# Two PSUM banks handed out by hand, centring ahead of the last masked score, and the variance inside a feature tile

## The chip, the core and the metric

The kernel runs on one core of a Trainium2 chip. Five engines work from queues of their own, each in order: TensorE (PE in the profile, its weight loads PEld), VectorE (DVE), ScalarE (ACT), GpSimd (POOL) and SyncE (SP), which here only issues DMAs. They wait for each other through semaphores. The metric is the time on the device in microseconds (us), the median of several runs. Matrix products accumulate in PSUM; a PSUM bank here is a tile of 128 partitions by 512 fp32 values.

## The reference

Attention over 8 batches of 8 heads with 576 tokens and head size 64, in which only scores close to the row's maximum count, and then a feed-forward block with a layer norm in front. All in fp32 (the feed-forward weights come in as float64):

```python
scores = matmul(q, k^T) / 8
keep   = scores >= max(scores) - tau
attn   = exp(scores - max(scores)) where keep, else 0
x      = concat_heads((attn / sum(attn)) @ v)               # (8, 576, 512)
mu, var = mean(x), mean((x - mu)**2)                        # over the 512 features
out    = x + max(((x - mu) / sqrt(var + 1e-6) * g_ln) @ w_ch1, 0) @ w_ch2
```

`w_ch1` is 512 x 2048, `w_ch2` 2048 x 512.

## The kernel before

**Slots and groups.** The attention runs in 72 slots, nine to a batch: for each pair of heads two slots of 256 queries, and one (the fifth) for the last 64 queries of all heads. The feed-forward block runs in 16 groups of 288 tokens, two to a batch (even group first). `x` lies with features on partitions, so a group's input is four chunks of 128 x 288. Program order is order on every engine (`tc.manual_schedule()`, L147); there is no scheduler that moves anything afterwards. The main loop (L1089) writes out a slot in four quarters, and `second_part(n, i)` (L1006) puts as many steps of the feed-forward generator between them as a budget allows. So TensorE's queue is one stream, in which products of both halves alternate.

**A slot.** `scores` (L388) fills two score tiles, VectorE takes negated maxima (L419), ScalarE exponentials (L432, four of 128 x 576), VectorE masks and sums each (L439, four, `weights`), POOL divides (L455), VectorE transposes (L529), and the result goes through a DRAM scratch tile and back (`turn_blocks`, `fetch`) and is multiplied with V in the next slot (L598, L608). Each of the two score tiles is three banks long (L376).

**Two more banks.** All other products use one pool, `ps_ff`, with one tag and two buffers (L76): whoever asks for a tile gets the buffer that was handed out longest ago, and waits until all that used it is done. In the feed-forward half they are, in order:

- `mean_of(g)` (L659): one product with a matrix of 1/512, which gives the mean in all partitions. While a group's segments run, a flag holds it back, and it is issued 12 steps into the last segment (L962 to L966).
- `centre(g)` (L666): VectorE subtracts the mean from the four chunks (L673) and so writes `xc`, which the first products of the group read. For an odd group this stands at the end of a slot, for an even one in the third quarter, behind all masked scores. At which quarter these are called is set in `group_ready` (L1036).
- `first_part(g)` (L776): 16 tiles of the hidden layer, each of four products into one bank (`p1`), which ScalarE empties with a relu (L796). On the way ScalarE squares `xc`, POOL adds up the squares, and after a later tile one product with the same matrix gives the variance (L809), from which ScalarE makes the inverse root: a bias row (L816), Ln (L817), Exp (L818). VectorE refines it (`root`, L734).
- `second_quarters` (L842) for groups 1 to 15: the second product by a scheme with seven products of half size; each of the seven segments fills a bank in 32 steps, and ScalarE copies it out (L887). Group 0 has a plain second product (`second_plain`).

The two lines that hand out a tile and hold the mean back:

```python
    ps_ff = ctx.enter_context(tc.tile_pool(name="ps_ff", bufs=2, space=bass.MemoryType.PSUM))   # L76
        for _ in range(12):                                                                     # L962
            yield next(last)
```

In the first slots (batch 0) the weights are still being converted from float64 by all engines, and the attention's transposes (`tp`, `tr`) and products with V (`pv`) use the same two banks.

Of the kernel before, what the change touches and what calls it, by code (L numbers as in the profile page):

```python
# [18 lines left out]
def kernel(  # L19
# [53 lines left out]
    dram = ctx.enter_context(tc.tile_pool(name="dram", bufs=3, space=bass.MemoryType.DRAM))  # L73
    ffn = ctx.enter_context(tc.tile_pool(name="ffn", bufs=2))
    ps_sc = ctx.enter_context(tc.tile_pool(name="ps_sc", bufs=1, space=bass.MemoryType.PSUM))
    ps_ff = ctx.enter_context(tc.tile_pool(name="ps_ff", bufs=2, space=bass.MemoryType.PSUM))  # L76

    tau_sb = consts.tile([128, 1], F32, name="tau_sb")
    scl_sb = consts.tile([128, 1], F32, name="scl_sb")
# [351 lines left out]
                yield es, thr  # L431
            nc.scalar.activation(es[:, i], blocks[i], func=AF.Exp, bias=neg[:, i : i + 1])  # L432

    def weights(es, thr, divide):


        den = small.tile([128, 4], F32, tag="den", name="den")
        for i in range(4):
            nc.vector.scalar_tensor_tensor(  # L439
                out=es[:, i], in0=blocks[i], scalar=thr[:, i : i + 1], in1=es[:, i],  # L440
                op0=ALU.is_ge, op1=ALU.mult, accum_out=den[:, i : i + 1],
            )
# [26 lines left out]
    def turn_weights(s, es, diags):  # L469


        em, er = turned_tiles(s)
        for i in range(4):
            if i:
                yield
            tp = ps_ff.tile([128, J, 128], F32, tag="ff", name="tp")
            for c in range(J):
                product(
                    tp[:, c], lhsT=es[:, i, c * 128 : (c + 1) * 128], rhs=diags[i],
                    start=True, stop=True,  # L480
                )
            if s == HP:
                nc.scalar.copy(
                    em[:, :, :, 32 * i : 32 * i + 32].rearrange("p a c x -> p c a x"),
                    tp.rearrange("p c (a x) -> p c a x", a=4),
                )
            else:
                h, j = divmod(i, 2)
                nc.scalar.copy(  # L489
                    em[:, 2 * j : 2 * j + 2, :, 64 * h : 64 * h + 64].rearrange("p a c x -> p c a x"),  # L490
                    tp.rearrange("p c (a x) -> p c a x", a=2),
                )
        tr = ps_ff.tile([128, 2, 128], F32, tag="ff", name="tr")
        for i in range(4):
            rest = es[:, i, J * 128 :]
            if s == HP:
                to = tr.rearrange("p a (b x) -> p (a b) x", b=2)[:, i]
                for half in range(2):
                    at = slice(64 * half, 64 * half + 64)
                    nc.tensor.matmul(to[at], lhsT=rest, rhs=diags[i][:, at], start=True, stop=True)  # L500
            else:
                h, j = divmod(i, 2)
                nc.tensor.matmul(
                    tr[64 * j : 64 * j + 64, h], lhsT=rest, rhs=diags[i], start=True, stop=True
                )
# [66 lines left out]
    def values_of(b, s, turned_weights):  # L572
# [2 lines left out]
        at_once = b == 0 and s <= HP  # L575
        pv = pv_behind
        if at_once:
            both = ps_ff.tile([128, 2, 128], F32, tag="ff", name="pv")
            pv = [both[:, j] for j in range(2)]
        if s == HP:  # L580
            outs = [
# [77 lines left out]
    def mean_of(g):  # L659
        if banks_taken[0]:  # L660
            waiting_mean.append(g)
            return
        means[g] = ps_ff.tile([128, TOK], F32, tag="ff", name="mean")
        product(means[g], lhsT=avg_sb, rhs=sums.pop(g), start=True, stop=True)

    def centre(g):  # L666
        nonlocal issued
        while waiting_mean:
            issued += next(queue[0])[1]
        xc = centred[g] = ffn.tile([128, NK, TOK], F32, tag="xc", bufs=1, name="xc")  # L670
        mean = means.pop(g)
        for c in range(NK):
            nc.vector.tensor_tensor(  # L673
                out=xc[:, c], in0=groups[g][:, c], in1=mean, op=ALU.subtract
            )

# [99 lines left out]
    def first_part(g):  # L776
# [6 lines left out]
        for d in range(ND):  # L783
            while conversion.carried < 4 * (d // 4 + 1):
                yield 0, 0
            while d == ND - 2 and len(rooted) <= g and not plain:
                run_all(aside)
            p1 = ps_ff.tile([128, TOK], F32, tag="ff", name="p1")
            for c in range(NK):
                product(  # L790
                    p1, lhsT=w1_sb[c][:, d * 128 : (d + 1) * 128], rhs=xc[:, c],
                    start=(c == 0), stop=(c == NK - 1),
                )
                if c < NK - 1:
                    yield 1, 1
            nc.scalar.activation(hidden[:, d], p1, func=AF.Relu)  # L796
            next(sums_of, None)
            yield 2, 1
            if sq is None and d and (part > 1 or d == ND // 2 - 1):
# [2 lines left out]
                nc.scalar.activation(sq, xc, func=AF.Square)  # L802
                for c in range(1, NK):
                    nc.gpsimd.tensor_tensor(out=sq[:, 0], in0=sq[:, 0], in1=sq[:, c], op=ALU.add)
            elif sq is not None and rb is None and (
                d >= squared + (7 if plain else 3) and part > (0 if plain else 1)
                or d == ND - NK - 1
            ):
                var = ps_ff.tile([128, TOK], F32, tag="ff", name="var")  # L809
                product(var, lhsT=avg_sb, rhs=sq[:, 0], start=True, stop=True)  # L810
                rb = ffn.tile([128, TOK], F32, tag="rb", bufs=2, name="rb")
                two = [sq[:, c] for c in (2, 3)]
                if plain:
                    two = [ffn.tile([128, HM, HT], F32, tag="part", bufs=4, name="two") for _ in two]
                    two = [t.rearrange("p m t -> p (m t)") for t in two]
                nc.scalar.activation(two[0], var, func=AF.Identity, bias=eps_sb)  # L816
                nc.scalar.activation(rb, two[0], func=AF.Ln)  # L817
                nc.scalar.activation(rb, rb, func=AF.Exp, scale=-0.5)  # L818
                aside.append(lambda: root(rb, *two))
                yield 1, 1  # L820
        for _ in sums_of:
            pass
        return rb

    def second_plain(g, rb):
        for m in range(NK):
            p2 = ps_ff.tile([128, TOK], F32, tag="ff", name="p2")
            for d in range(ND):
                while conversion.carried <= conversion.n1 + 4 * m + d // 4:
                    yield 0, 0  # L830
# [11 lines left out]
    def second_quarters(g, rb):  # L842
# [29 lines left out]
                eng.tensor_tensor(out=out[at], in0=in0[at], in1=in1[at], op=op)  # L872

        def segment(weights, rhs, out=None):
            bank = ps_ff.tile([128, HM, HT], F32, tag="ff", name="seg")
            for d in range(HD):
                for m in range(HM):
                    at, end = (d, m), (HD - 1, HM - 1)
                    product(
                        bank[:, m], lhsT=weights[:, m, d], rhs=rhs[:, d],  # L880
                        start=at == (0, 0), stop=at == end,
                    )
                    if at != end:
                        yield 2, 0.5
            if out is None:
                out = ffn.tile([128, HM, HT], F32, tag="part", bufs=4, name="part")
            nc.scalar.copy(out, bank)  # L887
            return out

        def last_tiles(weights, rhs):  # L890


            for m in range(HM):
                bank = ps_ff.tile([128, HT], F32, tag="ff", name="end")
                for d in range(HD):
                    product(
                        bank, lhsT=weights[:, m, d], rhs=rhs[:, d],
                        start=d == 0, stop=d == HD - 1,
                    )
# [4 lines left out]
                dve.tensor_tensor(out=z, in0=bank, in1=rb[:, late], op=ALU.mult)  # L904
# [54 lines left out]
            later(("hi", 3, finish, pool, 1))  # L959
        yield 2, 0.5  # L960
        last = last_tiles(s4, b22) if ends_here else segment(s4, b22)
        for _ in range(12):  # L962
            yield next(last)
        banks_taken[0] = False
        while waiting_mean:
# [70 lines left out]
    def group_ready(g):  # L1036
# [3 lines left out]
            at_quarter(*before, lambda: among.append(g))  # L1040
        else:
            at_quarter(*before, mean_of, g)
            at_quarter(*(first if g and first[1] else before), centre, g)
        at_quarter(*first, lambda: queue.append(ffn_steps(g)))

    conversion = Weights()
# [18 lines left out]

    def constants(times):

        warm = ps_ff.tile([128, QH], F32, tag="ff", name="warm")
# [20 lines left out]
    for n in range(NS):  # L1089
# [43 lines left out]
        if n > FIRST:  # L1133
            conversion.prepare_to(behind_at, False)
        blocks_go = by_blocks(n)
        diags = weights(es, thr, blocks_go)
        run_all(aside)
        drip()
        if n < SLOTS:
# [97 lines left out]
```

## Time and profile before

| | |
|---|---|
| three timed runs | 1346.41, 1346.46, 1348.77 us; median 1346.46 |
| span of the profiled execution | 1345.5 us |
| TensorE busy | 1313.5 us (98%) |
| VectorE busy | 870.6 us (65%) |
| POOL busy | 621.9 us (46%) |
| ScalarE busy | 458.7 us (34%) |
| granted TensorE clock, mean | 0.998 |

The span goes from the first to the last instruction of one profiled execution. A line of a group reads: engine, line of the kernel, operation, output<-input, shape. A matrix product of the kernel (`product`, L96) is two instructions for the two halves of the output partitions, and the trace has two rows for each, so four rows are one product. The ends of TensorE's rows are modelled; what one row takes from the next is the distance between starts. Lines of waits read: who waited for whom, microseconds in total, how often, the longest.

### The profile page before, as it was taken

To read this page: it belongs to the slowest core of one execution; us is meant where nothing else is said; L and a number is where in the kernel's file an instruction comes from. 1 tells how busy PE (TensorE), PEld (TensorE's weight loads), DVE (VectorE), ACT (ScalarE), POOL (GpSimd) and SP (SyncE) were. 2 spreads that over 40 slices of the span, in tenths; PEclk is the share of its full clock that TensorE was granted. 3 is DMA by queue.
4 is the path that set the end of the run, shared out by engine and by line. 5 is a ranking of instruction groups with operands and counts; after the bars stand their busy time and mean duration, and the time that the engine had idled before them with its cause. 6 is when DMAs were issued, how large, how long until landed. Compare 5 with 4: busy or idle time off the path is not lost.

```text
span 1345.5 us, 40255 instructions
## 1 busy us (share of the span) xinstructions
PE 1313.5 (98%) x17304; PEld 989.7 (74%) x17304; DVE 870.6 (65%) x1544; ACT 458.7 (34%) x995; POOL 621.9 (46%) x836
## 2 busy tenths in 40 slices
PE   8898899999999999999999999999999999999997
PEld 7665567769686776868778696877869677786957
DVE  7879886667666675666756677656756667666112
ACT  5866333232323233232233324233232323333120
POOL 3475556534444444445535454443444445335312
PEclk9999999999999999999999999999999999999999
DMA  8937874557643775447734576447754476443211
GB/s 173 297 95 176 209 191 151 178 163 190 176 146 132 182 200 158 151 156 200 191 127 150 167 183 191 139 137 196 198 167 152 126 196 179 136 157 124 81 19 20
DMA packets 335298, 213.92 MB, mean 159 GB/s; under 512 B 247376, under 2 KB 292688, under 8 KB 327056
## 3 DMA queue, kind: packets, MB, share of 16 engines
q1 hardware_dynamic: 329008, 210.46, 54.6%
q8 instruction: 136, 2.23, 0.7%
q10 hardware_dynamic: 5952, 0.74, 0.4%
q0 software_dynamic: 160, 0.15, 0.1%
q14 instruction: 42, 0.34, 0.1%
HBM read 124.00 MB, written 87.29 MB: 157 GB/s over the span
## 4 chain that ended last, share of the span: by engine, by line
PE 91%; ACT 3%; DVE 2%; DMA 1%; POOL 1%; issue 1%; SPq 1%; POOLq 0%; ACTq 0%; DVEq 0%
PE p L101 38%; PE seg L101 31%; PE sc L405 10%; PE sc L598 9%; PE sc L608 2%; ACT e L432 1%; PE tp L101 1%; DVE e L439 1%; POOL w L308 1%; PE var L101 1%; PE mean L101 1%; SPq L118 0%; DMA scr<-et 0%; ACT em L489 0%; DMA k_in<-in_k_dram 0%
## 5 line engine op out<-in xcount | busy, mean ns | idle before, releaser
L101 PE MATMUL p<-xc,w 128*64 128x288 f32 x4096 | 517.1, 408 | 6.5 <-ACT part L887 4.6
L101 PEld LDWEIGHTS p<-xc,w 128*64 128x64 f32 x4096 | 287.7, 137 | 213.8 <-issue 13.5
L419 DVE TENSOR_REDUCE neg<-sc 128x2 f32<-128x1152 f32 x144 | 188.7, 1351 | 282.2 <-PE sc L405 281.6
L455 POOL TENSOR_SCALAR e<-e,den 128x576 f32<-128x576 f32 x264 | 205.9, 792 | 131.3 <-DVE den L444 131.3
L101 PE MATMUL seg<-hidden,w 128*64 128x144 f32 x3840 | 247.9, 287 | 0.0
L101 PEld LDWEIGHTS seg<-hidden,w 128*64 128x64 f32 x3840 | 234.9, 137 | 11.5 <-issue 8.5
L439 DVE SCALAR_TENSOR_TENSOR e<-sc,thr,e 128x576 f32<-128x576 f32 x288 | 222.4, 810 | 19.3 <-POOL thr L423 11.6
L423 POOL TENSOR_SCALAR thr<-neg,low_sb 128x2 f32<-128x2 f32 x144 | 39.4, 274 | 384.1 <-DVE neg L419 382.4
L796 ACT ACTIVATE hidden<-p 128x288 f32<-128x288 f32 x256 | 106.5, 416 | 305.3 <-PE p L101 303.7
L432 ACT ACTIVATE e<-sc,neg 128x576 f32<-128x576 f32 x288 | 197.6, 754 | 2.4 <-DVE neg L419 2.4
L529 DVE STREAM_TRANSPOSE et<-e 128x1152 f32<-128x1152 f32 x118 | 161.1, 1373 | 14.2 <-POOL e L455 13.7
L405 PE MATMUL sc<-kT,qT 64*64 64x384 f32 (+3 forms) x2048 | 140.3, 403 | 3.1 <-DVE e L439 3.1
L598 PE MATMUL sc<-em,v_in 128*64 128x128 f32 (+1 forms) x2368 | 130.9, 264 | 2.4 <-DVE w L293 2.4
L598 PEld LDWEIGHTS sc<-em,v_in 128*64 128x64 f32 x2368 | 124.0, 138 | 10.9 <-DVE w L293 2.6
L101 PE MATMUL seg<-hidden,stage 128*64 128x144 f32 x1920 | 123.3, 286 | 0.0
L101 PEld LDWEIGHTS seg<-hidden,stage 128*64 128x64 f32 x1920 | 117.6, 137 | 2.9 <-issue 2.9
L621 ACT COPY x<-sc 128x128 f32<-128x128 f32 x120 | 31.6, 265 | 245.2 <-PE sc L405 176.3
L405 PEld LDWEIGHTS sc<-kT,qT 64*64 64x64 f32 x2048 | 76.3, 133 | 44.6 <-issue 21.3
L872 POOL TENSOR_TENSOR hidden<-hidden 128x576 f32<-128x576 f32 x60 | 84.8, 1427 | 52.0 <-ACT hidden L796 42.4
L887 ACT COPY part<-seg 128x288 f32<-128x288 f32 x74 | 29.8, 403 | 190.6 <-PE seg L101 190.1
L872 DVE TENSOR_TENSOR hidden<-hidden 128x576 f32<-128x576 f32 x60 | 51.2, 887 | 51.5 <-PE seg L101 48.5
L101 PE MATMUL seg<-hidden,e 128*64 128x144 f32 x896 | 61.2, 286 | 0.0
(130 smaller groups left out, 1041.2 us busy)
## 6 DMA issues: line engine op xcount, KB each, us to landing
scr<-et SPq DMA_DIRECT2D x63, 1152.0 KB, 4.8
em<-scr SPq DMA_DIRECT2D x63, 1024.0 KB, 5.7
out_dram<-ot SPq DMA_DIRECT2D x248, 36.0 KB, 3.8
q_in<-in_q_dram SPq DMA_DIRECT2D x120, 72.0 KB, 2.7
er<-scr SPq DMA_DIRECT2D x132, 64.0 KB, 5.2
k_in<-in_k_dram SPq DMA_DIRECT2D x116, 72.0 KB, 3.0
v_in<-in_v_dram SPq DMA_DIRECT2D x28, 256.0 KB, 5.4
w<-in_moe_w_ch_dram SPq DMA_DIRECT2D x10, 512.0 KB, 7.0
```

Source lines behind the costliest of these rows:

```text
L101: nc.tensor.matmul(out[r], lhsT=lhsT[:, r], rhs=rhs, **flags)
L405: nc.tensor.matmul(sc[h][64 * i : 64 * i + 64, at : at + n], lhsT=ql[r] if s == HP else qT[r, half, j * 128 + 64 * i : j * 128 + 64 * i + 64],
L419: nc.vector.tensor_reduce(out=neg[:, i], in_=pairs[h], axis=AXL.X, op=ALU.max, negate=True,)
L423: nc.gpsimd.tensor_scalar(out=thr[:, i], in0=neg[:, i], scalar1=-1.0, scalar2=low_sb, op0=ALU.mult, op1=ALU.add,)
L432: nc.scalar.activation(es[:, i], blocks[i], func=AF.Exp, bias=neg[:, i : i + 1])
L439: nc.vector.scalar_tensor_tensor(out=es[:, i], in0=blocks[i], scalar=thr[:, i : i + 1], in1=es[:, i], op0=ALU.is_ge, op1=ALU.mult, accum_o ...
L455: nc.gpsimd.tensor_scalar(out=es[:, i], in0=es[:, i], scalar1=den[:, i : i + 1], scalar2=1.0, op0=ALU.mult, op1=ALU.mult,)
L529: nc.vector.transpose(et[:, :, 64 * h : 64 * h + 64].rearrange("p n (j c) -> p j n c", j=2), es[:, 2 * h : 2 * h + 2].rearrange("p j (n c) ...
L598: nc.tensor.matmul(dst[64 * h : 64 * h + 64], lhsT=vt[:, h, c, :], rhs=pick(em[:, 2 * j : 2 * j + 2, c], h), start=c == 0 and first, stop= ...
L621: nc.scalar.copy(x_of(2 * b + (s > HP))[:, s % (HP + 1), 128 * j : 128 * j + 128], pv[j])
L796: nc.scalar.activation(hidden[:, d], p1, func=AF.Relu)
L872: eng.tensor_tensor(out=out[at], in0=in0[at], in1=in1[at], op=op)
```

## The change

- The two banks become two fixed tiles, `ff`, and a list `ff_order` says which is handed out next. `bank()` hands out the first of the list and puts it at the end, as the pool did. `next_bank(t)` puts the bank of `t` first again, so that the next tile gets the same bank as `t`.
- `centre(g)` calls `next_bank(mean)` for groups from 2 on: the first `p1` of the group gets the mean's bank, and no longer that of the last segment.
- The variance is taken in the middle of the next feature tile, after two of its four products, and hands its bank on in the same way. The bias row follows at once; Ln and Exp come behind that tile's relu.
- For even groups from 2 on, the subtractions are called from inside `weights`, ahead of the last of the four masked scores.
- The mean of an even group is issued 8 steps into the last segment of the odd group before it, not 12.

```diff
-    ps_ff = ctx.enter_context(tc.tile_pool(name="ps_ff", bufs=2, space=bass.MemoryType.PSUM))
+    ps_ff = ctx.enter_context(tc.tile_pool(name="ps_ff", bufs=1, space=bass.MemoryType.PSUM))
+
+    ff = [ps_ff.tile([128, 512], F32, name=f"ff{i}") for i in range(2)]
+    ff_order = [0, 1]
+
+    def bank(*shape):
+
+        b = ff_order.pop(0)
+        ff_order.append(b)
+        if len(shape) == 1:
+            return ff[b][:, : shape[0]]
+        return ff[b][:, : shape[0] * shape[1]].rearrange("p (a c) -> p a c", a=shape[0])
+
+    def next_bank(t):
+
+        b = [x.tensor.name for x in ff].index(t.tensor.name)
+        ff_order.remove(b)
+        ff_order.insert(0, b)
...
-    def weights(es, thr, divide):
+    def weights(n, es, thr, divide):
         den = small.tile([128, 4], F32, tag="den", name="den")
         for i in range(4):
+            if i == 3:
+                run(n, "mask")
             nc.vector.scalar_tensor_tensor(
...
-        means[g] = ps_ff.tile([128, TOK], F32, tag="ff", name="mean")
+        means[g] = bank(TOK)
         product(means[g], lhsT=avg_sb, rhs=sums.pop(g), start=True, stop=True)
...
                 out=xc[:, c], in0=groups[g][:, c], in1=mean, op=ALU.subtract
             )
+        if g > 1:
+            next_bank(mean)
...
-            p1 = ps_ff.tile([128, TOK], F32, tag="ff", name="p1")
+            p1 = bank(TOK)
+            then = []
             for c in range(NK):
                 product(
                     p1, lhsT=w1_sb[c][:, d * 128 : (d + 1) * 128], rhs=xc[:, c],
                     start=(c == 0), stop=(c == NK - 1),
                 )
+                if c == NK // 2 - 1 and sq is not None and rb is None and (
+                    d > squared + (7 if plain else 3) and part > (0 if plain else 1)
+                    or d == ND - NK
+                ):
+                    var = bank(TOK)
+                    product(var, lhsT=avg_sb, rhs=sq[:, 0], start=True, stop=True)
+                    next_bank(var)
+                    rb = ffn.tile([128, TOK], F32, tag="rb", bufs=2, name="rb")
+                    two = [sq[:, c] for c in (2, 3)]
...
+                    nc.scalar.activation(two[0], var, func=AF.Identity, bias=eps_sb)
+                    then.append(lambda: nc.scalar.activation(rb, two[0], func=AF.Ln))
+                    then.append(lambda: nc.scalar.activation(rb, rb, func=AF.Exp, scale=-0.5))
+                    yield 1, 1
                 if c < NK - 1:
                     yield 1, 1
             nc.scalar.activation(hidden[:, d], p1, func=AF.Relu)
+            if then:
+                run_all(then)
+                aside.append(lambda: root(rb, *two))
...
-            elif sq is not None and rb is None and (
-                d >= squared + (7 if plain else 3) and part > (0 if plain else 1)
-                or d == ND - NK - 1
-            ):
-                var = ps_ff.tile([128, TOK], F32, tag="ff", name="var")
-                product(var, lhsT=avg_sb, rhs=sq[:, 0], start=True, stop=True)
-                rb = ffn.tile([128, TOK], F32, tag="rb", bufs=2, name="rb")
...
-                nc.scalar.activation(two[0], var, func=AF.Identity, bias=eps_sb)
-                nc.scalar.activation(rb, two[0], func=AF.Ln)
-                nc.scalar.activation(rb, rb, func=AF.Exp, scale=-0.5)
-                aside.append(lambda: root(rb, *two))
-                yield 1, 1
...
-        for _ in range(12):
+        for _ in range(12 if g % 2 == 0 else 8):
             yield next(last)
...
-            at_quarter(*(first if g and first[1] else before), centre, g)
+            at_quarter(*((first[0], "mask") if g and first[1] else before), centre, g)
...
-        diags = weights(es, thr, blocks_go)
+        diags = weights(n, es, thr, blocks_go)
```

All other tiles of the old pool (`tp`, `tr`, `pv`, `p2`, the segments and the last tiles) are taken from `bank()` in the same way.

More of the change, by code (lines that the diff above doesn't have):

```diff
@@ L475, in turn_weights @@
                 yield
-            tp = ps_ff.tile([128, J, 128], F32, tag="ff", name="tp")
+            tp = bank(J, 128)
             for c in range(J):
@@ L492, in turn_weights @@
                 )
-        tr = ps_ff.tile([128, 2, 128], F32, tag="ff", name="tr")
+        tr = bank(2, 128)
         for i in range(4):
@@ L577, in values_of @@
         if at_once:
-            both = ps_ff.tile([128, 2, 128], F32, tag="ff", name="pv")
+            both = bank(2, 128)
             pv = [both[:, j] for j in range(2)]
@@ L793, in first_part @@
                 )
+                if c == NK // 2 - 1 and sq is not None and rb is None and (
[7 more added lines that the diff above has]
+                    two = [sq[:, c] for c in (2, 3)]
+                    if plain:
+                        two = [ffn.tile([128, HM, HT], F32, tag="part", bufs=4, name="two") for _ in two]
+                        two = [t.rearrange("p m t -> p (m t)") for t in two]
+                    nc.scalar.activation(two[0], var, func=AF.Identity, bias=eps_sb)
+                    then.append(lambda: nc.scalar.activation(rb, two[0], func=AF.Ln))
+                    then.append(lambda: nc.scalar.activation(rb, rb, func=AF.Exp, scale=-0.5))
+                    yield 1, 1
                 if c < NK - 1:
@@ L804, in first_part @@
                     nc.gpsimd.tensor_tensor(out=sq[:, 0], in0=sq[:, 0], in1=sq[:, c], op=ALU.add)
-            elif sq is not None and rb is None and (
-                d >= squared + (7 if plain else 3) and part > (0 if plain else 1)
-                or d == ND - NK - 1
-            ):
-                var = ps_ff.tile([128, TOK], F32, tag="ff", name="var")
-                product(var, lhsT=avg_sb, rhs=sq[:, 0], start=True, stop=True)
-                rb = ffn.tile([128, TOK], F32, tag="rb", bufs=2, name="rb")
[L812 to L818, printed above, removed]
-                aside.append(lambda: root(rb, *two))
-                yield 1, 1
         for _ in sums_of:
@@ L826, in second_plain @@
         for m in range(NK):
-            p2 = ps_ff.tile([128, TOK], F32, tag="ff", name="p2")
+            p2 = bank(TOK)
             for d in range(ND):
@@ L874, in segment @@
         def segment(weights, rhs, out=None):
-            bank = ps_ff.tile([128, HM, HT], F32, tag="ff", name="seg")
+            seg = bank(HM, HT)
             for d in range(HD):
@@ L879, in segment @@
                     product(
-                        bank[:, m], lhsT=weights[:, m, d], rhs=rhs[:, d],
+                        seg[:, m], lhsT=weights[:, m, d], rhs=rhs[:, d],
                         start=at == (0, 0), stop=at == end,
@@ L886, in segment @@
                 out = ffn.tile([128, HM, HT], F32, tag="part", bufs=4, name="part")
-            nc.scalar.copy(out, bank)
+            nc.scalar.copy(out, seg)
             return out
@@ L893, in last_tiles @@
             for m in range(HM):
-                bank = ps_ff.tile([128, HT], F32, tag="ff", name="end")
+                end = bank(HT)
                 for d in range(HD):
                     product(
-                        bank, lhsT=weights[:, m, d], rhs=rhs[:, d],
+                        end, lhsT=weights[:, m, d], rhs=rhs[:, d],
                         start=d == 0, stop=d == HD - 1,
@@ L903, in last_tiles @@
                 z = ffn.tile([128, HT], F32, tag="part", bufs=4, name="z")
-                dve.tensor_tensor(out=z, in0=bank, in1=rb[:, late], op=ALU.mult)
+                dve.tensor_tensor(out=z, in0=end, in1=rb[:, late], op=ALU.mult)
                 add(dve, y12[:, m], y12[:, m], z)
@@ L1066, in constants @@
     def constants(times):
-        warm = ps_ff.tile([128, QH], F32, tag="ff", name="warm")
+        warm = bank(QH)
         for _ in range(times):
```

## The prediction

> **What bounds the kernel now.** I read the page first, then who waited for whom on TensorE, then the chain and the order in time around the three places that the change touches.
>
> ```profile
> PE 1313.5 (98%) x17304; PEld 989.7 (74%) x17304; DVE 870.6 (65%) x1544; ACT 458.7 (34%) x995; POOL 621.9 (46%) x836
> ...
> PEclk9999999999999999999999999999999999999999
> ```
>
> ```profile
> PE p L101 <- POOL w L308: 5.6, 3, 4.1
> PE p L101 <- ACT part L887: 4.6, 8, 0.6
> PE sc L405 <- DVE e L439: 3.5, 7, 0.9
> ```
>
> TensorE is busy for 98% of the span at a full clock, and all its recorded waits together are some 25 us, most of them in the first 175 us. Only one kind comes back later: eight waits of 0.57 us, in which the first product of a feature group waits until ScalarE has copied the last segment's bank (L887). Nothing but TensorE's own gaps can shorten this kernel. Here is one of the eight, the start of group 4 (TensorE, then VectorE, then ScalarE; columns: start, length, what, and in brackets the idle time before it):
>
> ```profile
> 410.57 0.66 PE L101 MATMUL seg<-hidden,e 128*64 128x144 f32 x8
> 411.06 0.66 PE L101 MATMUL mean<-sum,avg_sb 128*64 128x288 f32 x4
> 411.54 1.15 PE L101 MATMUL seg<-hidden,e 128*64 128x144 f32 x16
> 413.27 3.13 PE L101 MATMUL p<-xc,w 128*64 128x288 f32 x24 [0.57 <-ACT part L887]
> ```
>
> ```profile
> 410.25 0.82 DVE L439 SCALAR_TENSOR_TENSOR e<-sc,thr,e 128x576 f32<-128x576 f32 x1
> ...
> 410.99 0.81 DVE L439 SCALAR_TENSOR_TENSOR e<-sc,thr,e 128x576 f32<-128x576 f32 x1
> ...
> 411.93 1.53 DVE L673 TENSOR_TENSOR xc<-x,mean 128x288 f32<-128x288 f32 x4
> ```
>
> ```profile
> 409.58 0.43 ACT L887 COPY part<-seg 128x288 f32<-128x288 f32 x1
> 412.81 0.40 ACT L887 COPY part<-seg 128x288 f32<-128x288 f32 x1 [2.80 <-PE seg L101]
> ```
>
> Four rows are one product. A segment product comes every 0.245 us (two from 410.57 to 411.06), a 288-wide one every 0.485 (411.06 to 411.54). So the first feature product was due at 411.54 + 4 x 0.245 = 412.52 and came at 413.27: 0.75 us lost, more than the bracket says, since the recorded ends overlap. Row by row, the first half of a product after a stop takes 0.29 instead of 0.24, another 0.05: 0.80 in all.
>
> The variance has a smaller gap that the list of waits leaves out:
>
> ```profile
> 431.11 0.66 PE L101 MATMUL var<-hidden,avg_sb 128*64 128x288 f32 x4
> 431.79 4.10 PE L101 MATMUL p<-xc,w 128*64 128x288 f32 x32
> ```
>
> ```profile
> 431.33 0.41 ACT L796 ACTIVATE hidden<-p 128x288 f32<-128x288 f32 x1 [1.19 <-PE p L101]
> 431.90 0.50 ACT L816 ACTIVATE hidden<-var,eps_sb 128x288 f32<-128x288 f32 x1 [0.16 <-PE var L101]
> 432.43 0.44 ACT L817 ACTIVATE rb<-hidden 128x288 f32<-128x288 f32 x1
> 432.90 0.44 ACT L818 ACTIVATE rb<-rb 128x288 f32<-128x288 f32 x1
> ```
>
> 431.79 - 431.11 = 0.68, where a product takes 0.485: 0.19 is lost while the next tile waits for the relu of the tile before the variance (to 431.74), plus the same 0.05. All 15 groups after group 0 show this to within 0.01.
>
> **The change part by part.** Set against each other in full, the two instruction orders hold the same instructions. Only these move: the mean's product ahead of four segment products (groups 2, 4 .. 14), the four subtractions ahead of the last masked score (the same seven slots), the variance behind two more products (16 groups), and on ScalarE one relu ahead of Ln and Exp. POOL's and SP's orders are equal, so no DMA is moved past another.
>
> *Start of groups 4, 6 .. 14.* The first product now takes the mean's bank. It no longer waits for the copy (done at 413.21), but for all four subtractions, since they read that bank; in the changed order it waits for VectorE alone. They stand where the last masked score stood, 410.99, so they end at 410.99 + 1.53 = 412.52; with the 0.06 from an end to the next engine's start (copy 413.21, product 413.27) the product starts at 412.58, against 412.52 due: 0.06 left, and the 0.05 of a stop. The mean must be there for it: four products earlier is 411.06 - 0.98 = 410.08. Its bank is copied out until 410.01. But the mean waits for two engines, and where a product does that (323.12 to 323.23, row by row) it starts 0.11 after the first wait ends: 410.05 + 0.11 = 410.16, so 0.08 lost and about 0.03 for the stop. Gain 0.80 - 0.11 - 0.11 = 0.58 each, six times: 3.5. The best end, with no wait left, is 6 x 0.80 = 4.8. The worst: VectorE starts nothing before the recorded end of the operation ahead: 411.07 + 4 x 0.45 = 412.87, product at 412.93, gain 0.80 - 0.46 - 0.11 = 0.23 each, 1.4. I take 3.5, since masked scores follow each other after 0.74 for a length of 0.82 and the subtractions after 0.37 for 0.45 in these very rows. On that the Trainium skill has a rule against the change: "VectorE: DVE Perf Modes", "The DRAIN you can't avoid", says that the next operation doesn't start until the pipe is empty. Read strictly, that is the worst end, and the sum would be 1341.3 instead of 1339.2; the rows above disagree with it for operations that don't depend on each other.
>
> *Bank or columns.* In the rows of now the product (413.27) starts while VectorE still reads the mean (to 413.46), in another bank. If one bank allowed that, only the first subtraction would count and the 0.11 behind it would go: 0.7 more in all, 1338.5. The Trainium skill, "PSUM — Partial Sum Buffer", "PSUM bank collisions raise a hardware error", asks to guard a bank as a whole; no run here shows what happens otherwise.
>
> *Group 2.* Its masked scores come later against TensorE: the last at 253.30, so 253.30 + 1.52 + 0.06 = 254.88 against 254.84 now: 0.04 lost (bounds: 0.8 gained with no wait, 0.4 lost by the worst end). *Group 15.* No scores are left, its subtractions end at 1278.92; from the mean's bank the product comes at 1278.98 instead of 1278.88: 0.10 lost. *Odd groups 3 .. 13.* Nothing: the subtractions end at 333.23, scores lie between, and the product comes at 335.77.
>
> *The delayed masked score.* It ends 1.45 later, so POOL's last two divisions end about 0.9 later and the second transpose of that slot 0.4 later. Behind it on VectorE are sums of the segment stage, and behind those the scratch write and the fetch of the turned weights, which SP issues. The fetched weights lie ready at least 4.4 us before TensorE reads them in every slot from 250 us on, and the scores' banks are free long before 420: cost nothing. Without that cover it is 7 x 0.4 = 2.8.
>
> *Variance.* Set the tile that follows it at 431.11. Two products: variance at 432.08; its bank needs the relu that ends at 431.74, 0.3 to spare. Now the bias row started 0.13 after the variance's end (431.77 to 431.90); the same gives 432.87 to 433.37. The tile after takes this bank and is due at 431.11 + 5 x 0.485 = 433.54: 0.11 to spare after the 0.06. The relu comes at 433.75, Ln and Exp end at 435.1, ahead of the next relu (435.7). So 0.24 x 15 = 3.6 is gained; if the stop's 0.05 stays, 2.85; nothing, if the bias row comes 0.35 later than this. VectorE's Newton step began at 434.72 and now waits until 435.2; behind it are output transposes, nothing that TensorE waits for.
>
> *Group 0.* Idle 0.71 before the variance and 0.64 after it. Behind ScalarE's weight conversions the new order should save 0.4, and TensorE is on the chain there until 122 us; then come POOL's weights, for which it waits 4.1. I take 0.3, between 0 (swallowed) and 1.35 (both gaps gone).
>
> Sum: 3.5 + 3.6 + 0.3 - 0.04 - 0.10 = 7.3. The profiled execution has a span of 1345.5; the median, 1346.46, is 1.0 above it, and I take the gain from the median: 1339.2.
>
> **The rivals.**
> Subtractions that come no earlier: if the mean, at 410.16, or something on VectorE holds them at 411.93, the product waits for 413.46 + 0.06 = 413.52, 0.25 later than now, and the mean's 0.11 is paid: 6 x 0.36 = 2.2 lost; with the other parts 1344.9. For it: the mean now sits close behind ScalarE's copy. Against: it has 0.3 in hand, ending about 410.9 with its last row.
> Variance for nothing: the bias row comes too late for the next tile: 1346.46 - 3.7 = 1342.8. For it: only 0.11 in hand. Against: no exponential lies on ScalarE from 1.4 before to 4.8 after the variance in groups 1 to 15.
> Slower: the next tile now hangs on the bias row in ScalarE's queue. If a pair of exponentials (0.75 each) stood ahead of it, each of 15 groups would wait 1.5 - 0.11 = 1.4 instead of 0.24, 17 us lost, 1360 with the other parts' gain. It decides from a bias row about 0.6 late (15 x 0.5 eats the 7.3). Against it the same rows as above.
>
> **How the numbers follow.** This kernel's times lie within 0.2% (2.7 us), so less than that counts as no change. Forecast 0.75, subtractions no earlier 0.07, variance for nothing 0.11, slower 0.07. The forecast's own bounds are 1346.46 - (4.8 + 3.6 + 1.35) = 1336.7 and 1346.46 - (1.4 + 2.85 - 0.5) = 1342.7; that all good ends meet is unlikely, so the range is 1337.2 to 1343.0, which takes in the second rival. Faster 0.75 + 0.11 = 0.86, same 0.07, slower 0.07.
>
> **What would show it.** TensorE's list loses "ACT part" waits; in their place come at most small ones on VectorE's subtractions at groups 2 and 15. First products come some 0.06 after due in groups 4 to 14, a tile after the variance without a gap, the mean about 0.1 late. TensorE's recorded idle time falls by some 3.5 us, and its busy time by as much, since recorded ends overlap again where a stop goes. A mean that waits longer for its bank, a bias row late on ScalarE, or subtractions spaced wider than 0.37 would make this wrong.

## The result and the profile after

The changed kernel takes 1339.04 us in the median (five runs, 1338.81 to 1339.53), the kernel before, in five runs that include the three shown above, 1347.01 (1346.41 to 1348.77): a ratio of 0.9943 with a 95% interval of 0.9932 to 0.9955. On another chip it was 0.9949 (0.9935 to 0.9963). The prediction was 1339.2.

The page of the changed kernel and its list of who waited for whom on TensorE, whose tiles are now all called `ff`:

```profile
span 1337.5 us, 40245 instructions
...
PE 1310.3 (98%) x17304; PEld 996.2 (74%) x17304; DVE 872.5 (65%) x1544; ACT 457.7 (34%) x995; POOL 624.7 (47%) x836
```

```profile
PE ff L118 <- POOL w L325: 5.6, 3, 4.1
PE ff L118 <- DVE xc L692: 2.6, 4, 0.7
```

The eight waits for ScalarE's copy are gone. Four waits on the subtractions are in the list; those of groups 2 and 15 (0.63 and 0.67) have taken the place of the copy, the other two lie in batch 0. Group 4's start, on TensorE, VectorE and ScalarE:

```profile
408.72 0.71 PE L118 MATMUL ff<-sum,avg_sb 128*64 128x288 f32 x4
409.23 2.16 PE L118 MATMUL ff<-hidden,e 128*64 128x144 f32 x32
411.19 0.69 PE L118 MATMUL ff<-xc,w 128*64 128x288 f32 x4
```

```profile
408.81 0.81 DVE L458 SCALAR_TENSOR_TENSOR e<-sc,thr,e 128x576 f32<-128x576 f32 x1
...
409.55 1.54 DVE L692 TENSOR_TENSOR xc<-x,ff 128x288 f32<-128x288 f32 x4
411.01 0.81 DVE L458 SCALAR_TENSOR_TENSOR e<-sc,thr,e 128x576 f32<-128x576 f32 x1
```

```profile
408.14 0.44 ACT L912 COPY part<-ff 128x288 f32<-128x288 f32 x1
411.50 0.40 ACT L912 COPY part<-ff 128x288 f32<-128x288 f32 x1 [2.92 <-PE ff L118]
```

The eight segment products from 409.23 end at 409.23 + 8 x 0.245 = 411.19, and the first feature product starts at 411.19: nothing is lost there, and the copy comes after it. The subtractions start in place of the last masked score and end at 411.09. The mean's bank is copied out until 408.58, and the mean starts at 408.72, where 408.64 was due.

The variance of group 4, on TensorE and ScalarE:

```profile
429.99 0.66 PE L118 MATMUL ff<-hidden,avg_sb 128*64 128x288 f32 x4
430.47 3.08 PE L118 MATMUL ff<-xc,w 128*64 128x288 f32 x24
```

```profile
429.23 0.41 ACT L834 ACTIVATE hidden<-ff 128x288 f32<-128x288 f32 x1 [1.18 <-PE ff L118]
430.77 0.50 ACT L828 ACTIVATE hidden<-ff,eps_sb 128x288 f32<-128x288 f32 x1 [1.12 <-PE ff L118]
431.66 0.41 ACT L834 ACTIVATE hidden<-ff 128x288 f32<-128x288 f32 x1 [0.39 <-PE ff L118]
431.96 0.43 ACT L829 ACTIVATE rb<-hidden 128x288 f32<-128x288 f32 x1
```

From the variance to the next product it is 430.47 - 429.99 = 0.48, one product's time, and the tile after that runs on without a gap.

To see where the time went, each product of one kernel was paired with the same product of the other, since their order is the same but for means and variances. What the distance between the two grows by is the gain at that place:

```
place                                             predicted      measured
group starts 4, 6 .. 14: the mean                 -0.11 each     -0.14 each
                         the first product        +0.69 each     +0.80 each   (all of it)
group 2                                           -0.04          -0.06
group 15                                          -0.10          -0.09
variance, groups 2 to 15                          +0.24 each     +0.24 each
variance, group 1                                 +0.24          +0.25, and lost again at 193 us
variance, group 0                                 +0.30          +0.40, and lost again by 158 us
sum                                               +7.3           +7.2   (6 x 0.655 + 14 x 0.243 - 0.15)
```

The two spans differ by more, 1345.5 - 1337.5 = 8.0. The rest came before the change does anything: the first feature product of group 0 stands at 79.94 before and at 78.94 after, with the same instructions up to it (an experiment below settles whose 1.0 that is). The stretch from there to the end of the span, 1265.6 before and 1258.5 after, leaves it out, and the experiments are compared by it. It has a spread of its own, though. In nine of the thirteen profiles of this study group 2's first product comes 174.9 to 175.0 after group 0's, or would but for its own gain or loss, yet in three others, whose instructions up to group 2's start are those of the changed kernel, it comes 0.6 to 0.8 later. The piece from the start of TensorE's last row to the end of the span lies between 7.2 and 7.7. So a difference of stretches is sure to about 1 us, while a difference of paired products repeats within some 0.03 from group to group; where the two disagree, the paired products decide.

### The profile page after: what moved, and what is told of

Its sections match the earlier page's. It is cut to its first block, busy times and chain, and to the rows that moved or that the text cites. A ratio compares the mean times of both kernels' runs of the same rounds, so it can differ in the third digit from the quotient of the medians.

```text
span 1337.5 us, 40245 instructions
## 1 busy us (share of the span) xinstructions
PE 1310.3 (98%) x17304; PEld 996.2 (74%) x17304; DVE 872.5 (65%) x1544; ACT 457.7 (34%) x995; POOL 624.7 (47%) x836
## 4 chain that ended last, share of the span: by engine, by line
PE 91%; ACT 2%; DVE 2%; SPq 2%; DMA 1%; POOL 1%; issue 1%; POOLq 0%; DVEq 0%; ACTq 0%
PE ff L118 70%; PE sc L422 10%; PE sc L617 9%; PE sc L627 2%; SPq L135 1%; ACT e L449 1%; POOL w L325 1%; DVE e L458 1%; DVE xc L692 0%; DMA v_in<-in_v_dram 0%; DVE neg L436 0%; DMA k_in<-in_k_dram 0%; DMA scr<-et 0%; DMA qk_room<-in_k_dram 0%; POOL e L474 0%
## 5 line engine op out<-in xcount | busy, mean ns | idle before, releaser
L118 PE MATMUL ff<-xc,w 128*64 128x288 f32 x4096 | 516.5, 407 | 2.8 <-DVE xc L692 2.0
L118 PEld LDWEIGHTS ff<-xc,w 128*64 128x64 f32 x4096 | 293.5, 137 | 199.9 <-issue 13.9
L118 PE MATMUL ff<-hidden,w 128*64 128x144 f32 (+1 forms) x4096 | 281.2, 294 | 5.7 <-POOL w L325 5.6
L118 PEld LDWEIGHTS ff<-hidden,w 128*64 128x64 f32 x4096 | 252.7, 137 | 31.0 <-issue 9.6
L834 ACT ACTIVATE hidden<-ff 128x288 f32<-128x288 f32 x256 | 106.8, 417 | 282.8 <-PE ff L118 278.9
L118 PE MATMUL ff<-hidden,stage 128*64 128x144 f32 x1920 | 123.3, 286 | 0.0
L118 PEld LDWEIGHTS ff<-hidden,stage 128*64 128x64 f32 x1920 | 117.6, 137 | 2.9 <-issue 2.9
L912 ACT COPY part<-ff 128x288 f32<-128x288 f32 x74 | 29.9, 404 | 191.2 <-PE ff L118 190.8
L118 PE MATMUL ff<-hidden,e 128*64 128x144 f32 x960 | 65.5, 286 | 0.0
```

Source lines behind the costliest of these rows:

```text
L118: nc.tensor.matmul(out[r], lhsT=lhsT[:, r], rhs=rhs, **flags)
```

## The experiments

**The variance alone** and **the mean's part alone.** Do the two parts add up?

```diff
 # e_var_only: the changed kernel without these
-        if g > 1:
-            next_bank(mean)
-        for _ in range(12 if g % 2 == 0 else 8):
+        for _ in range(12):
-            at_quarter(*((first[0], "mask") if g and first[1] else before), centre, g)
+            at_quarter(*(first if g and first[1] else before), centre, g)
 # e_mean_only: the changed kernel with the variance behind a finished feature tile, as before
```

> Only the variance part is done; the mean, the subtractions and the banks behind the mean are as before. The start of a run moves with its first loads, so beside the median the stretch from group 0's first feature product to the end of the span is compared: 1265.6 us before, 1258.6 in the changed kernel. My theory, the parts add up: groups 2 to 15 gain 0.243 each, groups 0 and 1 nothing, 3.4 in all: stretch 1262.2, median 3.4 below the kernel before. Rival, the variance's gain needs the other part (a product that comes earlier at the group's start): stretch 1264 or more.

> The other part alone: mean's bank, subtractions ahead of the last masked score, mean after 8 steps; the variance stands where it stood before. My theory: groups 4 to 14 gain 0.655 each (0.795 at the first product less 0.14 at the mean), group 2 loses 0.05, group 15 loses 0.10: 3.8 in all, stretch 1261.8. Rival, as on record in the prediction (0.58 each, the losses at mean and first product added): 3.3, stretch 1262.3. If the two parts help each other, both single gains together come to less than 7.0.

Measured: the variance alone 1343.60 against 1346.39 (ratio 0.9977, 0.9967 to 0.9987), stretch 1262.5; the mean's part alone 1342.76 against 1346.39 (0.9978, 0.9969 to 0.9987), stretch 1261.4. The first theory holds in both, by the groups: paired product by product, the mean's part gives 0.64 to 0.68 a group, as in the whole change, and the variance alone gives 0.245 in every group from 1 on. Group 1's gain makes up here for what batch 0 lost before it, and group 4's copy comes 0.28 later in this kernel. The gains of the stretches, 3.1 and 4.2, add up to 7.3, where the whole change has 7.1, but 0.3 of the 4.2 lies behind TensorE's last product. Up to that product the gains are 3.1 and 3.8, the whole change has 7.2, and the 0.28 of group 4 is the difference. So the parts are independent.

**Only the two fixed banks**, nothing moved and no bank kept:

> Only the two fixed banks, handed out in turn as the pool did; nothing is moved and no bank is kept, so the order of instructions on every engine is that of the kernel before. What differs are the waits: a product into a bank waits for the last reader alone, where the pool also waited for TensorE's own earlier work in some places of batch 0. My theory: no difference, 1265.6 within 0.5 from the first feature product to the end and the median within 0.2% of the kernel before. Rival: the first feature product came 1.0 us sooner in the changed kernel's profile because of these waits, so its first feature product stands near 78.9 and the median is 1.0 lower.

Measured: 1346.88 against 1346.34 (ratio 1.0003, 0.9994 to 1.0013), stretch 1265.8. That banks are handed out by hand is worth nothing in itself.

**The kernel before once more**, for its start:

> The kernel before once more, for one profile. Its first profile had the first feature product at 79.94, the changed kernel's at 78.94, with the same instructions up to there. My theory: that 1.0 lies in the first loads of one execution, and another profile of the same kernel has it at 78.8 to 79.4 and a span near 1344.5. Rival: it is the kernel's own, and it stands at 79.9 again.

Measured: the first feature product at 78.86, span 1344.5, stretch 1265.7. So the 1.0 belongs to the first loads of the one profiled execution of before: it is there whole when the scores' products run at 17 us (17.12 against 16.14). In the other profiles of this study, too, the first feature product stands between 78.8 and 79.3, but for one at 81.7.

**Without the mean's bank:**

```diff
-        if g > 1:
-            next_bank(mean)
```

> The changed kernel in all but one thing: the first feature product takes the bank of the last segment again, as before, while subtractions and mean stay early. My theory, the bank is what frees the product: in groups 4 to 14 it waits for ScalarE's copy again, 0.75 + 0.05, and the mean's 0.14 is still paid, groups 2 and 15 are 0.15 better: stretch 1258.6 + 4.8 - 0.15 = 1263.2. Rival, the earlier subtractions are what counts and the copy would be in time: stretch 1258.6, no wait on the copy in the list.

Measured: stretch 1263.5 (1344.42 us, one run). TensorE's waits, and group 4 on TensorE, of this kernel:

```profile
PE ff L118 <- ACT part L910: 4.5, 8, 0.6
```

```profile
409.67 0.71 PE L118 MATMUL ff<-sum,avg_sb 128*64 128x288 f32 x4
410.18 2.16 PE L118 MATMUL ff<-hidden,e 128*64 128x144 f32 x32
412.90 1.43 PE L118 MATMUL ff<-xc,w 128*64 128x288 f32 x10 [0.56 <-ACT part L910]
```

The eight waits for the copy are back although the subtractions are early: due at 410.18 + 8 x 0.245 = 412.14, the product came at 412.90. It is the bank that frees it. Paired with the changed kernel, each of the six groups loses 0.80, as the theory has it, and against the kernel before each start is 0.13 worse: the mean's loss without the gain.

**The subtractions behind the last masked score again:**

```diff
-            at_quarter(*((first[0], "mask") if g and first[1] else before), centre, g)
+            at_quarter(*(first if g and first[1] else before), centre, g)
```

> The changed kernel in all but one thing: the four subtractions stand behind the last masked score again, while the first product waits for them in the mean's bank. My theory: the subtractions of groups 2, 4 .. 14 start 0.94 later (one masked score 0.74, the reciprocal 0.2), and the product with them, 0.90 to 0.95 each with its 0.05 for the stop: 6.6 in all, stretch 1265.2, so the bank without the earlier subtractions is worse than no change to this part. Rival, the earlier mean is enough: stretch below 1261.

Measured: stretch 1265.4 (1346.37 us). Group 4 on TensorE and VectorE:

```profile
411.04 2.16 PE L118 MATMUL ff<-hidden,e 128*64 128x144 f32 x32
413.89 0.46 PE L118 MATMUL ff<-xc,w 128*64 128x288 f32 x2 [0.70 <-DVE xc L692]
```

```profile
411.36 0.81 DVE L458 SCALAR_TENSOR_TENSOR e<-sc,thr,e 128x576 f32<-128x576 f32 x1
...
412.30 1.54 DVE L692 TENSOR_TENSOR xc<-x,ff 128x288 f32<-128x288 f32 x4
```

The subtractions end at 412.30 + 1.54 = 413.84, and the product follows 0.05 later, where it was due at 413.00. The bank alone takes one wait away and puts another, slightly longer one in its place: paired with the kernel before, each of these six groups loses 0.26, group 2 loses 0.97 and group 15 0.09, 2.6 in all. With 0.7 that batch 0 took longer in this execution, little is left of the variance's 3.4. Bank and early subtractions are worth something together and nothing apart.

**The mean after 12 steps, and after 9:**

```diff
-        for _ in range(12 if g % 2 == 0 else 8):
+        for _ in range(12):                          # e_mean_12
+        for _ in range(12 if g % 2 == 0 else 9):     # e_mean_9
```

> The changed kernel with the mean of even groups after 12 steps again. My theory: subtractions called ahead of the last masked score stand in VectorE's queue until the mean is there, and the first product with them: 0.74 + 0.05 later in groups 4 to 14 than in the changed kernel, less the mean's own 0.14 that goes, so 4.0 to 4.7 in all, with 0.1 for group 2: stretch from the first feature product to the end 1262.4 to 1263.3. Rival, the place of the mean matters little, as 9 steps instead of 8 cost 0.08 a group: 1259.5.

> The changed kernel with the mean of even groups after 9 steps of the last segment instead of 8. My theory: the mean's own wait (0.14 each) goes, but the subtractions start when the mean is there, at about the same time as now, so that the first product comes at the same time and waits 0.10 to 0.15 itself: stretch from the first feature product to the end unchanged at 1258.5 within 0.5. Rival, as the prediction has it (both losses are paid one by one): 6 x 0.11 less, 1257.9.

Measured: stretch 1263.2 with 12 steps (1346.91 us), within the theory's range. Paired with the changed kernel, though, the first products of the six groups come 0.96 later at their place, where 0.79 was expected, and the mean gives back 0.13: 4.9 in all, of which a shorter end of the span hides 0.2. VectorE of that kernel at group 4 stands idle ahead of the subtractions, while the last masked score behind them could have run:

```profile
411.58 0.81 DVE L458 SCALAR_TENSOR_TENSOR e<-sc,thr,e 128x576 f32<-128x576 f32 x1
...
413.16 1.55 DVE L692 TENSOR_TENSOR xc<-x,ff 128x288 f32<-128x288 f32 x4 [0.76 <-PE ff L118]
```

With 9 steps the stretch is 1259.4 (1340.57 us), and by the stretch neither expectation holds. Group 4 on TensorE and VectorE:

```profile
409.79 0.65 PE L118 MATMUL ff<-sum,avg_sb 128*64 128x288 f32 x4
410.28 1.88 PE L118 MATMUL ff<-hidden,e 128*64 128x144 f32 x28
412.17 1.19 PE L118 MATMUL ff<-xc,w 128*64 128x288 f32 x8
```

```profile
410.46 0.09 DVE L458 DVE_READ_ACCUMULATOR e<-sc,thr,e 128x1 f32 x1
410.56 1.54 DVE L692 TENSOR_TENSOR xc<-x,ff 128x288 f32<-128x288 f32 x4
```

The mean's own wait is gone (0.15 gained in each group, paired with the changed kernel), but its last row ends at 410.44 and the subtractions start at 410.56 instead of 410.46, where their turn was. They end at 412.10, and the product, due at 410.28 + 7 x 0.245 = 411.99, comes at 412.17: 0.22 lost with the stop. That is 0.08 a group worse, 0.5 in six. The theory was right in kind, with the product's wait too small; the rival, a gain, is refuted. The other 0.4 of the stretch, measured against the 1258.5 of the changed kernel, is not in these groups: batch 0 took 0.6 longer and the end of the span 0.2 less. So between 8 and 9 steps one wait takes the place of another: after 8 the mean loses 0.14, after 9 the first product loses 0.22. Fewer than 8 were not tried.

**The bias row behind the relu:**

```diff
-                    nc.scalar.activation(two[0], var, func=AF.Identity, bias=eps_sb)
+                    then.append(lambda: nc.scalar.activation(two[0], var, func=AF.Identity, bias=eps_sb))
```

> The changed kernel with the bias row behind the relu of the tile in which the variance is taken, in one row with Ln and Exp, so that the variance's bank comes free later. My theory: the tile after that takes this bank and now waits for relu and bias row, some 1.2 each (due at 2.43 after the tile's start, the relu from 2.6, the bias row until 3.6): 15 x 1.2 = 18 slower than the changed kernel, stretch 1276 to 1277. Rival, the place of the bias row does not matter: 1258.5.

Measured: stretch 1276.5 (1357.23 us). Paired with the changed kernel, 1.12 is lost in each of groups 2 to 15 and 0.90 in group 1; another 1.4 is lost in group 0, which the expectation did not count. Group 4 on TensorE and ScalarE:

```profile
434.89 1.14 PE L118 MATMUL ff<-xc,w 128*64 128x288 f32 x8
436.94 2.16 PE L118 MATMUL ff<-xc,w 128*64 128x288 f32 x16 [0.90 <-ACT hidden L828]
```

```profile
436.08 0.41 ACT L834 ACTIVATE hidden<-ff 128x288 f32<-128x288 f32 x1 [2.01 <-PE ff L118]
436.39 0.49 ACT L828 ACTIVATE hidden<-ff,eps_sb 128x288 f32<-128x288 f32 x1
```

The bias row ends at 436.88 and the next tile starts at 436.94: that tile hangs on the bias row, as the prediction's slower rival had it. In the changed kernel the row ended 0.1 before it was needed; here it is one instruction further back in the queue, and the whole change turns into a loss of 10 us.

**A version that goes further:** group 2's subtractions ahead of the third masked score, and the mean of group 15 earlier.

```diff
-            if i == 3:
+            if i == (2 if n < 2 * SLOTS else 3):
                 run(n, "mask")
-        for _ in range(12 if g % 2 == 0 else 8):
+        for _ in range(12 if g % 2 == 0 and g + 2 < NG else 8):
```

> A version that goes further: group 2's subtractions stand ahead of the third masked score instead of the fourth, and group 15's mean, too, is issued after 8 steps. My theory: group 2's product (0.80 lost) comes 0.73 earlier, since the subtractions start where the third masked score stood (251.55 in the changed kernel's profile, the mean ends at 251.29) and the product is then due just before they end; group 15's subtractions end 0.98 earlier than the product's due time allows for, and its 0.84 goes. Together 1.5 to 1.6 less than the changed kernel. Rival: the delayed third masked score or the earlier mean makes a new wait of the same size, and the time stays at the changed kernel's.

> The changed kernel once more, on the chip of the other kernels of this call, so that the version that goes further is compared with it and not over two chips. Expected: 7.2 us below the kernel before by the parts (14 variances of 0.243, six group starts of 0.655, less 0.15), so 0.9947 of it. Rival, the whole 8.0 us by which the two spans differ belong to the change: 0.9941.

Measured on one chip: the version 1338.65 (1338.56 to 1339.09), the changed kernel 1339.66 (1339.46 to 1341.54), the kernel before 1346.96; ratios to the latter 0.9939 (0.9926 to 0.9951) and 0.9949 (0.9935 to 0.9963). The two intervals overlap, the single times of the two do not: 1.0 us less, where 1.5 to 1.6 were expected. Group 2 came as expected, 0.72 earlier. Its subtractions and first product in this version:

```profile
251.89 1.54 DVE L692 TENSOR_TENSOR xc<-x,ff 128x288 f32<-128x288 f32 x4
```

```profile
253.49 1.92 PE L118 MATMUL ff<-xc,w 128*64 128x288 f32 x14
```

Group 15 gained 0.49 instead of 0.84. Its mean came two products earlier instead of four, since in that slot it is asked for only then, whatever the flag allows; the subtractions end at 1270.30 and the product comes at 1270.35, with 0.18 idle. And in this profile group 14 lost 0.32: the first masked score of its slot started 0.82 after the maxima, where it is 0.47 or 0.48 in every other profile of the study and in every other even group of this one. The order in time names a sum on POOL as what released it, but that sum ended only after the score had started, so what held it stays open.

As for the changed kernel itself, it lies 7.3 us below the kernel before on this chip, which fits the 7.2 of the parts and not the 8.0 of the spans.

## Why the prediction was right

- **TensorE's own gaps are all there is.** Right: 7.2 of the 7.3 to 8.0 us between medians are gaps at the places named, and TensorE's recorded idle time (span less busy time) fell from 32.0 to 27.2, where 1.0 of the 4.8 lies in the first loads, and its busy time by 3.2; 3.5 each were forecast.
- **The sum, and some luck.** Forecast 7.3, found 7.2, but the terms were not that good: the 0.4 that groups 4 to 14 gave beyond the forecast stand against 0.3 in group 0 and 0.24 in group 1 that did not pay. Luck, too, is how close the median came (1339.04 against 1339.2): the forecast subtracts from 1346.46, while the median of the kernel before beside it is 1347.01, so that the gain there is 8.0, and 7.3 on the chip of the version that goes further.
- **Groups 4, 6 .. 14, forecast 0.58 each.** Right in mechanism, and 0.07 too low, 0.4 us in all. The step that was off is the sum "0.80 - 0.11 - 0.11". The mean did wait, and lost 0.14 rather than 0.11: its first row came 0.09 after due (408.72, 408.64; forecast 0.08), and the rest is the stop; the subtractions did start where the last masked score stood (409.55) and took 1.54. But the two losses do not add. The mean's delay moves everything behind it on TensorE, the due time of the first product too, and the 0.06 by which the subtractions would have been late is smaller than that. The product loses nothing.
- **How closely VectorE's operations follow each other.** The four subtractions took 1.54 in place and the masked scores still follow after 0.74. The rule of the Trainium skill, "VectorE: DVE Perf Modes", section "The DRAIN you can't avoid", that an operation starts only when the one before has left the pipe, read strictly, would have put the product 0.35 later; it is not seen in these rows. The section itself adds that a next operation that is not held starts earlier, which the prediction left out.
- **Wait for all four subtractions, not for one.** Right: with the subtractions late, the product starts 0.05 after the end of the fourth (413.84, 413.89), while in the kernel before it started in the other bank before that end. Whether the same bank would bear it was not tried.
- **Group 2 and group 15.** Forecast 0.04 and 0.10 lost, measured 0.06 and 0.09.
- **Variance.** Forecast 0.24 each, measured 0.243 in groups 2 to 15. The bias row started 0.12 after the variance's recorded end (430.65, 430.77; forecast 0.13), and the Newton step, counted from the same place of TensorE's stream, 0.28 later than before (forecast 0.48, 434.72 to 435.2). Group 1 was counted and did not pay. Its gain is there at 189.7 and gone at 193.3, where a product with V waits for the slot's last masked score, which had just been in time before. The feature products came sooner, the scores' side of that slot did not.
- **Group 0, forecast 0.3.** The gap shrank by 0.40, as worked out, and all of it was swallowed, the lower bound, but not where the prediction looked. Part went at 129 us, where a product with V now waits 0.28 for a masked score and did not wait before, and by 146 us nothing was left (some 0.3 that shows once more at 155 us is gone by 158). The wait for POOL's weights at 153 us is as long as before (4.08, 4.07): POOL's conversions ahead of it start 48.7 after the first feature product in both kernels (128.65 before, 127.66 after).
- **The delayed masked score costs nothing.** Right: no new wait on the turned weights shows beyond batch 0.
- **The rivals.** "Subtractions that come no earlier" is what the kernel with late subtractions shows: the bank alone makes a group's start worse (0.26, forecast 0.36). "Variance for nothing" is refuted by the 0.24 in each group. "Slower" is what the kernel with the bias row behind the relu shows, with a relu ahead of the bias row in place of exponentials. The nearest exponential to the variance in groups 1 to 14 of the kernel before ends 1.3 ahead of it, not 1.4.

## What to carry to other kernels

When one engine is busy for 98% of the span, compare the distances between its starts with what the same shape takes elsewhere: a gap of 0.24 us hid behind recorded ends that overlap, and fourteen of them were half of this gain. A product that may start when a buffer comes free has two or three last waits within a few tenths of each other; taking the last away pays only up to the next one, so a bank, an order on VectorE and the time of a small product had to be moved together: any two of them without the third lost 0.13 to 0.26 a group. Losses in one in-order stream overlap: a wait that comes earlier moves the due time of all that stands behind it.

## What the runs showed that was not expected

- A product that waits for two engines pays for it, somewhat more than forecast: the mean lost 0.14 in each of six groups, although the copy of its bank had ended 0.14 before it started (408.58, 408.72). In the trace the wait for the copy is an instruction of its own ahead of the mean's weight load, at 408.62; the weight load follows at 408.69. A product that waits for one engine, with no such instruction ahead, follows an end after 0.05 to 0.06 (413.84 to 413.89, 436.88 to 436.94). With 9 steps the mean has the same two waits, both over in time, and loses nothing.
- The first loads move a run by more than most parts of this change: the same instructions brought the first feature product at 78.8 to 79.3 us in eleven profiles, at 79.9 in one and at 81.7 in one.
- In three kernels (fixed banks alone, the variance alone, late subtractions) ScalarE's copy at group 4 came 0.28 later behind the segment's last product than in the kernel before; only in the first two did a product wait for it. The order in time names POOL's division as what released ScalarE's copy there, but its records do not end where the copy starts, and it is so in that group alone: the cause stays open.
